# A banded-attention and feed-forward kernel on one core: the output projection one unit later, its weights 192 bytes into longer slots, and one pair of staging tiles less

## The chip, the core and the metric

The kernel runs on one core of a Trainium2 chip. The core has a matrix engine (TensorE, "PE" in the profile; its weight loads have a row of their own, "PEld"), a vector engine (VectorE, "DVE"), ScalarE ("ACT"), GpSimd ("POOL") and SyncE ("SP"). Each works through its own list of instructions in order and waits for others on semaphores. PE, ACT and DVE also reach PSUM, eight banks in which matmuls accumulate; everything else lies in SBUF, 128 partitions wide. Transfers are issued from the lists of SP, POOL and ACT.

The metric is the device time of one execution in microseconds (us).

## The reference

Sequence 2048, width 640 (32 heads of 20), feed-forward width 1536, all in float32.

```python
xn = _layernorm(x)
q, k, v = split(xn @ wqkv)                    # 32 heads of 20
idx = pos - [0, 2, 4, ..., 14]                # 8 earlier positions, every second one
logits = einsum(q, k[idx]) * 20 ** -0.5       # positions before the start are masked
s = (softmax(logits) . v[idx]) @ wo
g = silu(silu(xn @ w1) @ w2)
return x + s * g
```

## The kernel before

**Groups.** The 2048 positions are cut into four groups of 512: two halves of the sequence, and in each the even and the odd positions apart, since attention looks back in steps of 2. A group is T = 4 tiles of 128 positions.

**Precision.** Each float32 operand of a matmul is split into a high and a low part of the type fp32r, and a product is three matmuls: high by high, low by high, high by low. TH and TL hold the transposed activations' parts ([128, DC = 5, 512] each, two of each); a weight unit holds both parts side by side.

**Units.** The weights come as units, in the order of the list `units` (lines 277 to 287): per group 20 of `q` (NQ = 4 quarters of 8 heads, 5 chunks of 128 input rows; 480 columns), from the second group on 5 of `wo` (640 columns), then `w1` f and `w2` f - 1 alternating, f to 11 (`w1` is the stationary operand there; `w2` has 640 columns, and its stationary operand is SH/SL, the activated hidden units). The last group's `wo` comes at the end, in `wo_last`. `WR` is a ring of RING = 7 slots of 2 x 640 floats. Unit i lies in slot i % 7; `w_done` behind a unit's matmuls calls `w_load` (line 349) for the unit seven further on. When a unit comes for the first time (for half the `q` units the second time too), it is loaded raw by `raw_load` (line 315) into staging tiles (`RAW`, at first also `PR` and `G`), split by ACT and DVE or POOL, and stored in split form to DRAM; after that it is fetched in split form by a POOL transfer. `start` (line 311) gives the place in the slot at which a unit begins: QAT = 48 floats (192 bytes) for `q`, 0 else.

**A group's phases.** `qkv_phase` (line 624): four quarters of matmuls, 60 each; ACT copies their four banks out (lines 444, 447); transfers on SP fetch the earlier positions (halo, line 458); DVE does the scores (lines 481, 484 to 494) and the values (503 to 521), a backlog that goes on for the whole group. Between the quarters `o_chunk` transposes the previous group's attention output O into TH/TL (PE line 433, ACT 437, DVE 438), five chunks, at the places of O_AT. `wo_phase` (line 690) multiplies that by Wo: c = 0..4, and for each c the four tiles, in six PSUM banks: a[t] with 384 columns of tile t, b[t // 2] with the other 256 of two tiles. DVE multiplies the six banks into the gate G (line 704) in the order a0, a1, b0, a2, a3, b1; then four residual tiles are fetched into the two tiles XR by SP, POOL adds G (line 711), SP stores the result. `ffn_phase` (line 766): per f a W1 unit into one of two ROT banks (PE 791 to 793), ACT's silu twice (797, 798), DVE's low part (799), and the W2 unit of f - 1 into six banks (PE 672, 674 in `tm_mm`): first all tiles' products with SH, then those with SL. After the last f, ACT puts silu of the six banks into G (line 828). The six banks of `tm_banks` (line 663) are the same six in Wo and W2, in the same order; the quarters use them too.

In the last group the five chunks of O are transposed inside `ffn_phase`, ahead of the f of OL_AT, and `wo_last` (line 715) follows.

**The order.** It isn't the order of the program text. Every operation is handed to `Weave` with an engine, a price and a priority, and `Weave.order` plays the program through on its own clock: PE keeps its order, and on every other engine the next operation is, of those that can start first, the one with the lowest number as priority. L704 and L799 have 0, the attention work 100 and more. After the six operations of L704 the plan keeps DVE free for HOLD = 3.4 us; no instruction comes of that. The order that results is fixed in the instruction lists. A matmul of n columns is priced at `mm(n) = n / 2400 + 0.0155` us, so a Wo or W2 unit at 12 x (mm(384) + mm(256)).

Of the kernel before, what the change touches and what calls it, by code (L numbers as in the profile page):

```python
# [9 lines left out]
F32R = mybir.dt.float32r  # L10
# [4 lines left out]
P = 128  # L15
S, D, F, H, DH = 2048, 640, 1536, 32, 20
W = 8
DC, FC = D // P, F // P
# [15 lines left out]
HALVES = 1  # L34
BY_ACT = (1,)
QAT = 48
X_AT = 3, 6, 8
TILE_AT = 1, 1.5, 5, 6
LOW_AT = 3
# [134 lines left out]
def local_attention_silu_ffn(ctx: ExitStack, tc: tile.TileContext, x, wqkv, wo, w1, w2, out):  # L174
# [25 lines left out]
    ST = [sb.tile([P, 2, 6], F32, name="st0")]  # L200
    TH = tiles("th", 2, [P, DC, TOK], F32R)
    TL = tiles("tl", 2, [P, DC, TOK], F32R)
    WR = tiles("w", RING, [P, 2 * D], F32R)
    ST.append(sb.tile([P, 2, 6], F32, name="st1"))
    SH = tiles("sh", 2, [P, TOK], F32R)
    SL = tiles("sl", 2, [P, TOK], F32R)
# [11 lines left out]
    G = sb.tile([P, T, D], F32, name="gate")  # L218
    XR = tiles("xr", 2, [P, D])
    SF = tiles("sf", 2, [P, TOK])  # L220
    RAW = tiles("raw", 2, [P, D])
    ACC = [psum.tile([P, TOK], F32, name=f"acc{i}") for i in range(6)]
    ROT = [psum.tile([P, TOK], F32, name=f"rot{i}") for i in range(2)]
    carry = [dram.tile([2, NQ, 2, T, CQ], F32, name=f"carry{par}") for par in range(2)]
# [52 lines left out]
    units = []  # L277
    for g in range(NG):
        units += [("q", q, c) for q in range(NQ) for c in range(DC)]
        if g:  # L280
            units += [("wo", c) for c in range(DC)]
        for f in range(FC + 1):
            if f < FC:
                units.append(("w1", f))
            if f:
                units.append(("w2", f - 1))
    units += [("wo", c) for c in range(DC)]
# [22 lines left out]

    def start(u):

        return QAT if u[0] == "q" else 0

    def raw_load(k):


        if k >= len(fresh):
            return
        i = fresh[k]  # L320
        u = units[i]
        n = width(u)
        if k < DC:
            r, kr = PR.rearrange("p t w m -> p (t w m)")[:, k * n:(k + 1) * n], [PRK[k]]
        elif k < early:
            s = (k - DC) % 6
            r, kr = (RAW[s], [("raw", s)]) if s < 2 else (G[:, s - 2, :], [("g", s - 2, 0), ("g", s - 2, CA)])
            r = r[:, :n]
        else:
            s = k % 2  # L330
            r, kr = RAW[s][:, :n], [("raw", s)]
        raws[i] = r, kr
        if u[0] == "q":
            _, q, c = u
            src = wqkv[c * P:(c + 1) * P, :].rearrange("p (s m) -> p s m", s=3)[:, :, q * CQ:(q + 1) * CQ]
            dst = r.rearrange("p (s m) -> p s m", s=3)
        elif u[0] == "w1":
            src = w1.rearrange("(c p) f -> p c f", p=P)[:, :, u[1] * P:(u[1] + 1) * P]
            dst = r.rearrange("p (c f) -> p c f", c=DC)
        else:  # L340
            m = wo if u[0] == "wo" else w2
            src, dst = m[u[1] * P:(u[1] + 1) * P, :], r
        if k in BY_ACT:
            add("ACT", 0.65, lambda: nc.scalar.dma_start(dst, src), [], kr, -1, nbytes=n * P * 4)
            return
        dma(lambda: nc.sync.dma_start(dst, src), [], kr, n * P * 4, 1 + k if k < 2 * DC else clock[0] + 5,
            0.62 if k < 2 * DC else 0.45)

    def w_load():
        i = loaded[0]  # L350
        if i >= len(units):
            return
        loaded[0] += 1
        u, s = units[i], i % RING
        n = width(u)
        r = WR[s]
        at = start(u)
        both = r.rearrange("p (s d) -> p s d", s=2)[:, :, at:at + n]
        whi, wlo = both[:, 0], both[:, 1]
        kh, kl = ("wh", s), ("wl", s)  # L360
        due = clock[0]
        if what[i] == "load":
            src = halves[u]
            add("POOL", 1.0, lambda: nc.gpsimd.dma_start(both, src), [("half", u)], [kh, kl], due + 10,  # L364
                nbytes=2 * n * P * 4)
            return
        k = fresh.index(i)
        if not k:
            raw_load(0)
            rawn[0] = 1  # L370
        raw, kr = raws.pop(i)
        act(n, lambda: nc.scalar.activation(whi, raw, AF.Copy), kr + [("sd", 0)] * (k < 2), [kh], 1000 + due)
        pool_does = k < LO and k not in ON_DVE
        eng, cost, by = ("POOL", po(n), nc.gpsimd) if pool_does else ("DVE", dv(n), nc.vector)
        parts = HALVES if pool_does and k < DC else 1
        for j in range(parts):
            cs = slice(j * n // parts, (j + 1) * n // parts)
            add(eng, po(n // parts) if pool_does else cost, lambda cs=cs: by.tensor_tensor(
                out=wlo[:, cs], in0=raw[:, cs], in1=whi[:, cs].bitcast(F32), op=OP.subtract), [kh] + kr,
                [kl if j == parts - 1 else kl + (j,)], due if pool_does else LOW_AT if k < LO else 50, lock=True)  # L380
        if what[i] == "store":
            kept = dram.tile([P, 2, n], F32, name="half_" + "_".join(map(str, u)))
            halves[u] = kept
            dma(lambda: nc.sync.dma_start(kept, both.bitcast(F32)), [kh, kl], [("half", u)], 2 * n * P * 4,
                due + 25)
        while rawn[0] <= (min(k + 6, early - 1) if k < early - 2 else k + 2):
            raw_load(rawn[0])
            rawn[0] += 1
# [268 lines left out]
        return [(k, i, c, t) for k in kinds for c in cs for t in ts]  # L657

    O_AT = {(1, 1): 0, (1, 4): 1, (2, 3): 2, (3, 1): 3, (3, 3): 4}
    OL_AT = {8: 0, 9: 1, 10: 2, 11: 3, 12: 4}  # L660
    XT_AT = 7

    def tm_banks():
# [102 lines left out]
    def ffn_phase(g, i, ix, io):  # L766
        nxt = g + 1 if g + 1 < NG else None
        ps = prev = None
        for f in range(FC + 1):
            if nxt is not None and f == 0:  # L770
                load_x(nxt, 0, 2)
                load_x(nxt, 2, 2)
                for t in range(T):
                    ln_stats(t)
                ln_rstd(0, T)
                for t in range(T):
                    ln_apply(t)
            if nxt is not None and XT_AT <= f < XT_AT + DC:
                split_t(XIN, [("xin", t) for t in range(T)], f - XT_AT, ix)
            if nxt is None and f in OL_AT:  # L780
                o_chunk(g, OL_AT[f], io)
            cur = None
            if f < FC:
                wh, wl, kh, kl = w_next("w1", f)
                h, kp = rot()
                s = f % 2

                def first(wh=wh, wl=wl, h=h):
                    for c in range(DC):
                        cs = tsl(c)  # L790
                        nc.tensor.matmul(h, wh[:, cs], TH[i][:, c, :], start=c == 0, stop=False)  # L791
                        nc.tensor.matmul(h, wh[:, cs], TL[i][:, c, :], start=False, stop=False)  # L792
                        nc.tensor.matmul(h, wl[:, cs], TH[i][:, c, :], start=False, stop=c == DC - 1)  # L793
                pe(15 * mm(TOK), first, t_keys(i, range(DC)) + [kh, kl], [kp])
                w_done()
                sf, sh, sl = SF[s], SH[s], SL[s]
                act(TOK, lambda sh=sh, h=h: nc.scalar.activation(sh, h, AF.Silu), [kp], [("sh", s)], 0, "silu")  # L797
                act(TOK, lambda sf=sf, h=h: nc.scalar.activation(sf, h, AF.Silu), [kp], [("sf", s)], 0, "silu")
                dve(TOK, lambda sf=sf, sh=sh, sl=sl: nc.vector.tensor_tensor(  # L799
                    out=sl, in0=sf, in1=sh.bitcast(F32), op=OP.subtract), [("sf", s), ("sh", s)], [("sl", s)], 0, lock=True)  # L800
                cur = sh, sl, ("sh", s), ("sl", s)
            if f:
                sh, sl, ksh, ksl = prev
                if ps is None:
                    ps = tm_banks()
                a, b = ps
                wh, wl, kh, kl = w_next("w2", f - 1)
                for t in range(T):
                    def big(t=t, f=f, wh=wh, wl=wl, sh=sh):
                        tm_mm(ps, t, sh[:, tsl(t)], wh, f == 1, False)  # L810
                        tm_mm(ps, t, sh[:, tsl(t)], wl, False, False)

                    def small(t=t, f=f, wh=wh, sl=sl):
                        tm_mm(ps, t, sl[:, tsl(t)], wh, False, f == FC)
                    ko = [a[t][1], b[t // 2][1]]
                    pe(2 * TM, big, [ksh, kh, kl], ko)
                    if f == FC:
                        pe(TM, small, [ksl, kh], ko)
                    else:
                        late.append((TM, small, [ksl, kh], ko))  # L820
                for args in late:
                    pe(*args)
                late.clear()
                w_done()
            prev = cur
# [8 lines left out]
    for g in range(NG):  # L834
        other = 1 - slot
        qkv_phase(g, slot, other)
        if g:
            wo_phase(g - 1, other)
        ffn_phase(g, slot, other, other)
        if g < NG - 1:  # L840
            slot = other
# [30 lines left out]
```

## Time and profile before

| | |
|---|---|
| three runs | 641.08, 641.5, 641.52 us (median 641.5) |
| the profiled execution | 641.25 us, span of the profile 639.5 us |
| matrix engine busy | 632.2 us |
| vector engine busy | 540.1 us |
| ScalarE, GpSimd busy | 204.1, 122.3 us |
| read from and written to device memory | 109.55 MB, 34.16 MB |

The profile page gives busy times, a chain of waits that ends with the last instruction, and the costliest groups of instructions. Its trace can be cut into windows, where a row gives the length of the stretch, the busy time of an engine, its instructions in brackets, the granted clock of the matrix engine, and the share and rate of the transfers. The trace can also be listed in order of time: start, duration, engine, line of the kernel, operation, what it writes and reads, and, in square brackets, how long the engine was idle before it and what ended that. Matmuls overlap, so the pace is read from start to start, not from the duration of one.

### The profile page before, as it was taken

The page shows a single profiled execution, that of the slowest core. Times are in us where ns is not written, and L with a number is a line of the kernel's source. Part 1 is how long each engine was busy: PE and PEld are TensorE (multiplying, and loading weights), DVE is VectorE, ACT ScalarE, POOL GpSimd, SP SyncE. Part 2 cuts the span into 40 slices and gives each one's busy share as a digit, 9 for nine tenths or more (in the row PEclk, how much of TensorE's full clock was granted, in tenths as well). Part 3 has the DMA queues.
Part 4 walks back from the last instruction along what each step waited for, and adds up shares of the span by engine and source line. Part 5 has one row for each costly group of instructions (what it writes and reads, how often), then busy time and mean ns, then how long its engine had stood idle before and what let it go on. Part 6 is the DMA issues. An engine that isn't in the chain of part 4 may idle for free.

```text
span 639.5 us, 9016 instructions
## 1 busy us (share of the span) xinstructions
PE 632.2 (99%) x3495; PEld 572.2 (89%) x3495; DVE 540.1 (84%) x539; ACT 204.1 (32%) x399; POOL 122.3 (19%) x168
## 2 busy tenths in 40 slices
PE   7999999999999999999999999999999999999997
PEld 6888889999889989999888999999988899899997
DVE  7699999999999899999859999999106999999714
ACT  5436453443524023232422112223313222233230
POOL 4500000001101241111222124311222213311100
PEclk9999999999999999999999999999999999999999
DMA  9999998787999998657699976965679996876522
GB/s 283 336 307 337 338 372 327 298 280 237 280 285 327 318 310 258 197 163 218 179 270 272 297 214 207 359 201 162 171 207 265 276 315 202 284 272 189 183 83 82
DMA packets 74154, 162.44 MB, mean 254 GB/s; under 512 B 5648, under 2 KB 47088, under 8 KB 74112
## 3 DMA queue, kind: packets, MB, share of 16 engines
q0 software_dynamic: 26672, 82.58, 44.7%
q1 hardware_dynamic: 46896, 78.88, 39.6%
q8 instruction: 27, 0.44, 0.3%
q10 hardware_dynamic: 544, 0.41, 0.2%
q14 instruction: 15, 0.12, 0.1%
HBM read 109.55 MB, written 34.16 MB: 225 GB/s over the span
## 4 chain that ended last, share of the span: by engine, by line
PE 97%; DVE 1%; DMA 1%; ACT 0%; issue 0%
PE acc L672 22%; PE acc L674 15%; PE acc L638 10%; PE acc L639 10%; PE acc L640 10%; PE rot L793 9%; PE rot L791 9%; PE rot L792 9%; PE rot L433 2%; PE acc L583 2%; DMA xin<-in_A_x_dram 1%; DVE st L548 1%; DVE xin L553 0%; PE rot L761 0%; PE rot L562 0%; DVE tl L570 0%
## 5 line engine op out<-in xcount | busy, mean ns | idle before, releaser
L638 PE MATMUL acc<-w,th 128*128 128x480 f32 x300 | 114.7, 382 | 0.0
L672 PE MATMUL acc<-w,sh 128*128 128x384 f32 x384 | 113.6, 335 | 0.0
L639 PE MATMUL acc<-w,tl 128*128 128x480 f32 x300 | 113.5, 378 | 0.0
L640 PE MATMUL acc<-w,th 128*128 128x480 f32 x300 | 113.4, 378 | 0.0
L674 PE MATMUL acc<-w,sh 128*128 128x256 f32 x384 | 107.1, 279 | 0.0
L481 DVE TENSOR_TENSOR pr<-q,kv 128x2560 f32<-128x2560 f32 x32 | 90.3, 2821 | 11.7 <-DMA kv<-kv 11.3
L791 PE MATMUL rot<-th,w 128*128 128x512 f32 x240 | 95.4, 398 | 0.0
L793 PE MATMUL rot<-th,w 128*128 128x512 f32 x240 | 94.0, 391 | 0.0
L792 PE MATMUL rot<-tl,w 128*128 128x512 f32 x240 | 93.8, 391 | 0.0
L513 DVE TENSOR_TENSOR pr<-e,kv 128x2560 f32<-128x2560 f32 x32 | 90.3, 2823 | 0.8
L484 DVE TENSOR_REDUCE l<-pr 128x128 f32<-128x2560 f32 x32 | 90.0, 2813 | 0.2
L364 POOL DMA_DIRECT2D w<-half_q x52 | 37.3, 717 | 233.4 <-PE rot L793 122.5
L518 DVE TENSOR_TENSOR pr<-pr 128x1280 f32<-128x1280 f32 x64 | 78.3, 1224 | 1.1
L797 ACT ACTIVATE sh<-rot 128x512 fp32r<-128x512 f32 x48 | 28.8, 599 | 151.5 <-PE rot L793 151.4
L674 PEld LDWEIGHTS acc<-w,sh 128*128 128x128 f32 x384 | 72.3, 188 | 1.6
L672 PEld LDWEIGHTS acc<-w,sh 128*128 128x128 f32 x384 | 72.1, 188 | 1.7
L364 POOL DMA_DIRECT2D w<-half_w x72 | 38.5, 535 | 182.0 <-PE acc L674 89.9
L640 PEld LDWEIGHTS acc<-w,th 128*128 128x128 f32 x300 | 56.3, 188 | 8.5
L638 PEld LDWEIGHTS acc<-w,th 128*128 128x128 f32 x300 | 56.3, 188 | 8.0
L639 PEld LDWEIGHTS acc<-w,tl 128*128 128x128 f32 x300 | 56.3, 188 | 8.0
L672 PE MATMUL acc<-w,sl 128*128 128x384 f32 x192 | 57.8, 333 | 0.0
L793 PEld LDWEIGHTS rot<-th,w 128*128 128x128 f32 x240 | 45.0, 188 | 9.9
(88 smaller groups left out, 975.0 us busy)
## 6 DMA issues: line engine op xcount, KB each, us to landing
w<-half_w POOLq DMA_DIRECT2D x72, 640.0 KB, 5.7
w<-half_q POOLq DMA_DIRECT2D x52, 480.0 KB, 5.4
half_w<-w SPq DMA_DIRECT2D x24, 640.0 KB
half_q<-w SPq DMA_DIRECT2D x20, 480.0 KB
w<-half_wo POOLq DMA_DIRECT2D x15, 640.0 KB, 5.5
kv<-kv SPq DMA_DIRECT2D x16, 560.0 KB
kv<-kv SPq DMA_DIRECT2D x16, 420.0 KB
gate<-in_B_w_dram SPq DMA_DIRECT2D x16, 320.0 KB
```

The costliest lines, as they stand in the source:

```text
L481: dve(2560, lambda t=t: nc.vector.tensor_tensor(out=PR, in0=win(qq[:, t:t + 2, :], W, 0), in1=win(kv[:, 0, t:t + 2, :], W, CQ), op=OP.mult ...
L484: dve(2560, lambda t=t: nc.vector.tensor_reduce(out=l[:, t:t + 2].rearrange("p t w h -> p (t w h)"), in_=PR.rearrange("p t w (h d) -> p (t ...
L513: dve(2560, lambda t=t, v=v: nc.vector.tensor_tensor(out=PR.rearrange("p t w (h d) -> p t (w h) d", d=DH), in0=e[:, t:t + 2].rearrange("p ...
L518: dve(2 * n * CQ, lambda n=n: nc.vector.tensor_tensor(out=PR[:, :, 0:n, :], in0=PR[:, :, 0:n, :], in1=PR[:, :, n:2 * n, :], op=OP.add), [] ...
L638: nc.tensor.matmul(o, hi, wh, start=c == 0, stop=False)
L639: nc.tensor.matmul(o, lo, wh, start=False, stop=False)
L640: nc.tensor.matmul(o, hi, wl, start=False, stop=c == DC - 1)
L672: nc.tensor.matmul(a[t][0][:, :CA], st, w[:, :CA], start=first, stop=last)
L674: nc.tensor.matmul(b[t // 2][0][:, h * CB:(h + 1) * CB], st, w[:, CA:], start=first and h == 0, stop=last, skip_group_check=True)
L791: nc.tensor.matmul(h, wh[:, cs], TH[i][:, c, :], start=c == 0, stop=False)
L792: nc.tensor.matmul(h, wh[:, cs], TL[i][:, c, :], start=False, stop=False)
L793: nc.tensor.matmul(h, wl[:, cs], TH[i][:, c, :], start=False, stop=c == DC - 1)
```

## The change

The five Wo units move behind W1 unit 0 of the next feed-forward phase, in the list of units and in the phases: `wo_phase` is called inside `ffn_phase` when f is 0, after W1 unit 0 and its activations are handed to the plan. The slots of the ring get 64 floats more (256 bytes; 1792 over the ring, by which the tiles allocated behind it move), and a Wo unit begins 48 floats into its slot, as a `q` unit does already. The two tiles RAW are gone; raw weights are staged in XR, the tiles of the residual. In the last group the fourth chunk of O is transposed one step later (f = 12) and the fifth in the middle of the last W2 unit, before its third tile.

```diff
+WOAT = 48
+SLOT = 2 * D + 64
...
-    WR = tiles("w", RING, [P, 2 * D], F32R)
+    WR = tiles("w", RING, [P, SLOT], F32R)
...
-    RAW = tiles("raw", 2, [P, D])
...
         units += [("q", q, c) for q in range(NQ) for c in range(DC)]
-        if g:
-            units += [("wo", c) for c in range(DC)]
         for f in range(FC + 1):
             if f < FC:
                 units.append(("w1", f))
+            if g and f == 0:
+                units += [("wo", c) for c in range(DC)]
             if f:
                 units.append(("w2", f - 1))
...
-        return QAT if u[0] == "q" else 0
+        return QAT if u[0] == "q" else WOAT if u[0] == "wo" else 0
...
-            r, kr = (RAW[s], [("raw", s)]) if s < 2 else (G[:, s - 2, :], [("g", s - 2, 0), ("g", s - 2, CA)])
+            r, kr = (XR[s], [("xr", s)]) if s < 2 else (G[:, s - 2, :], [("g", s - 2, 0), ("g", s - 2, CA)])
...
-            r, kr = RAW[s][:, :n], [("raw", s)]
+            r, kr = XR[s][:, :n], [("xr", s)]
...
-        both = r.rearrange("p (s d) -> p s d", s=2)[:, :, at:at + n]
+        both = r[:, at:at + 2 * D].rearrange("p (s d) -> p s d", s=2)[:, :, :n]
...
-    OL_AT = {8: 0, 9: 1, 10: 2, 11: 3, 12: 4}
+    OL_AT = {8: 0, 9: 1, 10: 2, 12: 3}
...
                 cur = sh, sl, ("sh", s), ("sl", s)
+                if g and f == 0:
+                    wo_phase(g - 1, io)
...
                 for t in range(T):
+                    if nxt is None and f == FC and t == T // 2:
+                        o_chunk(g, DC - 1, io)
...
         qkv_phase(g, slot, other)
-        if g:
-            wo_phase(g - 1, other)
         ffn_phase(g, slot, other, other)
```

## The prediction

> **What bounds the kernel now.** I read the page's busy shares and its chain of waits first, then the matrix engine (PE) cut into windows at the borders of the phases that move, then the vector engine (DVE) around the same places in order of time.
>
> ```profile
> PE 632.2 (99%) x3495; PEld 572.2 (89%) x3495; DVE 540.1 (84%) x539; ACT 204.1 (32%) x399; POOL 122.3 (19%) x168
> ...
> PE 97%; DVE 1%; DMA 1%; ACT 0%; issue 0%
> ```
>
> PE is never out of work: 632.2 of 639.5 us, and 97% of the chain. So the time changes only where matmuls follow each other faster or slower, or where a matmul starts to wait. DVE, at 84%, is the only other engine near its limit.
>
> The stretch of group 2 that moves: first Wo unit, Wo units 2 to 5, W1 unit 0, W1 unit 1, W2 unit 0 (after the colon-separated borders: length, PE busy, matmuls, clock, DMA share, GB/s):
>
> ```profile
> 358.54:362.23 3.69, 3.69 (x25) 1.00 1.17 397
> 362.23:376.31 14.08, 14.08 (x98) 1.00 1.13 294
> 376.31:379.74 3.43, 3.43 (x18) 1.00 0.64 202
> 379.74:383.14 3.40, 3.40 (x17) 1.00 0.10 36
> 383.14:386.59 3.45, 3.45 (x25) 1.00 0.33 124
> ```
>
> The clock is 1.00 throughout. A Wo unit takes 14.08/4 = 3.52 us, its first one 0.17 us more. A W2 unit, with the same 24 matmuls of 384 and 256 columns, takes 3.45. The same work, then, has two paces. Group 3 has the same shape; its Wo starts at 515.22 and its first W2 at 539.80. The last row is group 1 from Wo's end to its first W2:
>
> ```profile
> 515.22:518.92 3.70, 3.70 (x25) 1.00 1.07 335
> 518.92:533.00 14.08, 14.08 (x98) 1.00 0.99 285
> 533.00:539.80 6.80, 6.80 (x32) 1.00 0.44 139
> ...
> 219.65:226.45 6.80, 6.80 (x32) 1.00 0.84 276
> ```
>
> Now DVE beside these, groups 1, 2 and 3 (start, length, instruction):
>
> ```profile
> 218.94 3.14 DVE L704 TENSOR_TENSOR gate<-acc,gate 128x384 f32<-128x384 f32 x6
> ...
> 380.20 3.14 DVE L704 TENSOR_TENSOR gate<-acc,gate 128x384 f32<-128x384 f32 x6
> 383.26 0.77 DVE L799 TENSOR_TENSOR sl<-sf,sh 128x512 fp32r<-128x512 f32 x1
> 383.95 2.81 DVE L484 TENSOR_REDUCE l<-pr 128x128 f32<-128x2560 f32 x1
> ...
> 535.45 3.14 DVE L704 TENSOR_TENSOR gate<-acc,gate 128x384 f32<-128x384 f32 x6
> ...
> 540.71 2.81 DVE L484 TENSOR_REDUCE l<-pr 128x128 f32<-128x2560 f32 x1
> ```
>
> L704 is the multiplication that empties Wo's six banks. In group 2 Wo ends at 376.31, yet L704 starts only at 380.20, 3.89 us later; in group 3 at 533.00 and 535.45, 2.45 later; in group 1 before the end (219.65). DVE isn't idle in between: it works through an order that was fixed at build time by a plan in which PE is slower. The plan prices a W2 unit at 12 x (mm(384) + mm(256)) = 12 x 0.298 = 3.57 us, and the row above says 3.45. Over a group PE gets ahead of the plan, and whatever the plan put ahead of L704 then makes the banks late. Today this is harmless: the next user of the banks is the first W2 unit, two W1 units (6.83 us) behind Wo's end.
>
> **The change part by part.**
>
> *Wo's entry.* Today Wo's banks are those of the last quarter, and Wo waits for ScalarE to copy them out:
>
> ```profile
> PEld acc L674 <- ACT q L447: 0.8, 3, 0.3
> ...
> 62.94:66.37 3.43, 3.43 (x17) 1.00 1.12 364
> ```
>
> The first Wo unit is 0.17 to 0.18 us over the others, three times. With W1 unit 0 (own banks, 3.43 us) between, the copies are long done. W1 directly behind a quarter is what group 0 has: 3.43 (second row) against 3.40, so 0.03 is paid back. Sum: 3 x (-0.18 + 0.03) = **-0.45 us**.
>
> *The 192 bytes.* No added instruction; only the address at which the moving matrix starts against the stationary one. From the tile sizes in the code, W2's stationary tile lies 64 bytes (the small statistics tile between, rounded up) past a multiple of 256 from its weights, and for a quarter, whose weights start 192 in, the stationary tile is again 64 past a multiple of 256. Wo alone of the three sits at 0. That Wo has W2's shapes but not its pace fits. The bounds: W2's 3.45, and above it the slowest the same shapes ever run, the last W2 unit:
>
> ```profile
> 614.32:618.00 3.68, 3.68 (x27) 1.00 0.00 0
> ```
>
> Per phase of five units that is -0.35 to +0.80. I take -0.35, the row whose address relation Wo gets: four phases, **-1.40 us**.
>
> The Trainium skill speaks against it: SBUF — State Buffer, "Who interferes with whom", gives PE two independent read ports, one for the moving operand and one for weight loads, and says PE never waits on anyone for SBUF. By that rule the offset is worth 0. Here Wo and W2 differ by 2% at equal shapes and clock, which the rule does not explain, but nothing yet shows that the address is the reason.
>
> *The longer slots* move every second slot by 256 bytes against a multiple of 512, for W1, W2 and the quarters too. I take 0, since the relation modulo 256 is kept everywhere; the other end is among the rivals.
>
> *Wo's move: DVE.* This carries the forecast. In the plan Wo's sums are done one W1 unit, 3.43 us, later. Of DVE's work only one piece moves ahead of L704 with it: L799 of W1 unit 0, 0.69 us at a free engine. So the plan has 3.43 - 0.69 = 2.74 us more of waiting before L704 can be issued, and fills it from the attention work, in pieces of 2.81 us: in groups 2 and 3 the next in line is L484 (383.95, 540.71). However long the plan waited before (anything from 0 to one piece), one L484 goes ahead, unless it waited nearly a whole piece already. On the chip none of that is waited for, since PE is ahead; DVE simply reaches L704 later: 380.20 + 0.69 + 2.81 = 383.70 in group 2, 535.45 + 3.50 = 538.95 in group 3. Both places hang on PE's time, because DVE starts each of these groups by waiting for the halo of its first quarter:
>
> ```profile
> 330.98 2.83 DVE L481 TENSOR_TENSOR pr<-q,kv 128x2560 f32<-128x2560 f32 x1 [6.40 <-DMA kv<-kv]
> ...
> 485.84 2.83 DVE L481 TENSOR_TENSOR pr<-q,kv 128x2560 f32<-128x2560 f32 x1 [4.58 <-DMA kv<-kv]
> ```
>
> so a loss in group 2 doesn't save group 3 from its own. What is late next: W2 unit 0 is now one W1 unit behind Wo. Its order of need is a0, b0 (short matmul, 0.18 us in), later b1 (2 x 4 matmuls, 1.15 us, after b0); DVE's order is a0, a1, b0, a2, a3, b1. b0 is done half way, 1.57 us into L704, b1 at 3.14.
>
> Group 2: PE reaches b0 at 358.54 + 3.43 + 5 x 3.45 + 3.40 + 0.18 = 382.80; b0 is ready at 383.70 + 1.57 = 385.27: 2.47 us. b1 is wanted at 385.27 + 1.15 = 386.42 and ready at 386.84: 0.42. Together 2.89. Group 3: 515.22 + 3.43 + 17.25 + 3.58 = 539.48 against 538.95 + 1.57 = 540.52: 1.04, and 0.42 again: 1.46. Group 1: L704 slips by at most 0.69 + 2.74 + a piece, from 218.94 to 225.2 at the very latest, with b0 at 226.8; b0 is wanted at 226.45 - 0.15 - 0.35 + 0.18 = 226.1. The next pieces there are shorter (1.48, below), so some 223 is likelier: 0, at worst 0.7. Sum: **+4.35 us**. Lower end 0, if the plan finds no piece to put ahead; upper end: PE further ahead by another 0.5.
>
> Queued behind the waiting matmuls is all of PE, so nothing hides this.
>
> *Wo's move: POOL and SP.* Per group five weight loads, five stores once, four residual loads, adds and stores change place. POOL's order holds a weight load behind the residual adds, which wait for L704:
>
> ```profile
> 381.90 3.56 POOL L711 TENSOR_TENSOR xr<-xr,gate 128x640 f32<-128x640 f32 x2 [4.59 <-DVE gate L704]
> 385.41 1.10 POOL L364 DMA_DIRECT2D w<-half_w  x2
> ...
> w<-half_w POOLq DMA_DIRECT2D x72, 640.0 KB, 5.7
> ```
>
> L704 3.5 us later holds them 3.5 us longer. A load is issued seven slots ahead, six units of 3.4 us or more, 20 us, and lands in 5.7: 14 us of cover. 0; without that cover up to 3.5 per group.
>
> *Raw weights in XR.* The last raw tile is read at 206.17 and the first residual add is at 222.43; one unit later each, they stay apart. 0.
>
> ```profile
> 206.17 0.83 DVE L378 TENSOR_TENSOR w<-raw,w 128x640 fp32r<-128x640 f32 x1 [0.29 <-ACT w L372]
> ...
> 222.43 3.10 POOL L711 TENSOR_TENSOR xr<-xr,gate 128x640 f32<-128x640 f32 x2
> ```
>
> *The last two transposes* (five as before): one stood before a W1 unit, which then took 3.52 instead of 3.45; one before the last W2 unit, which took 3.68. Now both split the last W2 unit: 0.23 a piece at worst, +0.16 in all; since each slows only half a unit, 0.
>
> ```profile
> 606.99:610.51 3.52, 3.52 (x18) 1.00 0.64 195
> ```
>
> Sum: -0.45 - 1.40 + 4.35 = +2.50. The profiled execution took 641.25 us (span 639.5 and 1.75 around it), 0.25 under the median of the runs, 641.5. **641.25 + 2.50 = 643.8 us.**
>
> **Rivals.**
> - *No wait (the other side).* The plan had nearly waited a piece already, or holds DVE free for Wo's sums, and L704 goes right behind L799: 380.20 + 0.69 = 380.89, b0 at 382.46, before PE wants it at 382.80. Then 641.25 - 0.45 - 1.40 = **639.4**. It decides from where L704 starts in group 2 earlier than 382.80 - 1.57 = 381.2. For it: the plan prefers L704 to all attention work as soon as it can start. Against: the 3.89 us of today.
> - *Wo keeps its pace.* Then the waits shrink by 0.35 each, to 2.54 and 1.11, and -1.40 falls away: 641.25 - 0.45 + 3.65 = **644.5**. By the skill's two ports this is the likelier one.
> - *The slots' 256 bytes count.* If W2 runs at 3.68 in every second slot, 24 units x 0.23 = 5.5 more: **649**. For it: W2 has shown that pace; against: only behind transposes, in one place.
> - *Waits and gains cancel*, because the piece put ahead is a short one, as L518 in group 1 (1.48):
>
> ```profile
> 226.02 1.48 DVE L518 TENSOR_TENSOR pr<-pr 128x1280 f32<-128x1280 f32 x1
> ```
>
> L704 at 382.37, b0 at 383.94: 1.14 and 0.42; in group 3 only b1, 0.13. 641.25 - 1.85 + 1.69 = **641.1**. Against: no L518 is next in line in groups 2 and 3.
>
> **How the numbers follow.** Forecast 0.41, Wo's old pace 0.18, no wait 0.24, cancel 0.10, slots 0.07. A measurement of this kernel can tell 0.2%, 1.3 us, from no change. Slower (over 642.8): 0.41 + 0.18 + 0.07 = 0.66; the same 0.10; faster (under 640.2) 0.24. The range takes in the no-wait case and Wo's slow bound (+0.80 a phase cuts the waits to 1.74 and 0.3: 641.25 - 0.45 + 3.20 + 2.04 = 646.0): 639.3 to 646.0. The likeliest one's own range is 642.8 to 645.5.
>
> **What would show it.** In the changed profile: two PE waits on DVE's L704 at the first W2 unit of groups 2 and 3, 2 to 3 and 1 to 2 us, none in group 1; one L484 more ahead of L704; Wo units at 3.45; no wait for L447 at Wo's entry; W1, W2 and quarter units at 3.40 to 3.45 and their old pace. Wrong if L704 starts within 2 us of Wo's end in group 2, or if W2's units have two lengths.

## The result and the profile after

| | before | after |
|---|---|---|
| median of 12 runs (us) | 641.22 (640.95 to 642.86) | 642.60 (642.23 to 644.04) |
| ratio, 95% interval | | 1.0023 (1.0015 to 1.0031) |
| profiled execution, span (us) | 641.25, 639.5 | 642.30, 640.5 |

The change costs 1.4 us in the median and 1.0 in the profiled pair. The forecast was 643.8, 2.5 over the kernel before: the direction is right and the time lies inside the stated range (639.3 to 646.0), but 0.2 below the likeliest case's own range (642.8 to 645.5). The profile shows that the kernel gets there another way than was forecast.

First the busy line of the page of after:

```profile
PE 633.2 (99%) x3495; PEld 573.8 (90%) x3495; DVE 535.4 (84%) x539; ACT 211.8 (33%) x405; POOL 126.1 (20%) x168
```

Then all that the matrix engine (PE) waited for in after (line that waited and its releaser; us in all, times, longest):

```profile
PE rot L563 <- DVE xin L554: 1.8, 3, 0.9
PE rot L537 <- POOL ident masks.py:199: 1.4, 1, 1.4
PE acc L584 <- DVE tl L571: 0.3, 1, 0.3
```

PE's busy time is 1.0 us up (632.2 to 633.2), as much as the span, and its three waits are those of the program's start. No wait for the vector engine (DVE) at a W2 unit is among them. So the forecast's stall isn't there, and matmuls run slower somewhere. The windows of PE in after tell where: Wo in group 1; W1 unit 0, Wo, W1 unit 1, W2 unit 0 of group 2; Wo in group 3; Wo's last part (the matmuls of `wo_last`):

```profile
205.25:223.24 17.99, 17.99 (x121) 1.00 1.05 345
...
358.78:362.22 3.44, 3.44 (x16) 1.00 1.19 366
...
362.22:380.22 18.00, 18.00 (x122) 1.00 1.04 278
380.22:383.66 3.44, 3.44 (x17) 1.00 0.04 12
383.66:387.11 3.45, 3.45 (x25) 1.00 0.40 121
519.19:537.19 18.00, 18.00 (x122) 1.00 0.99 267
618.77:634.92 16.15, 16.15 (x107) 1.00 0.11 42
```

And the last part before:

```profile
618.00:633.83 15.83, 15.83 (x107) 1.00 0.11 42
```

A Wo phase was 17.77 (3.69 + 14.08), its entry wait of 0.18 included; now it is 18.00 without one. The last part went from 15.83 to 16.15. W2 unit 0 has its old 3.45, at full clock. Three phases by 0.22 and the last part's 0.32 make 0.98, about the difference of the spans.

Inside the phase, in after (start, length, instruction). A pair is a matmul of 384 columns and one of 256, and its pace, from here on, is the time from one start of L673 to the next:

```profile
362.22 0.34 PE L673 MATMUL acc<-w,th 128*128 128x384 f32 x1
362.40 0.28 PE L675 MATMUL acc<-w,th 128*128 128x256 f32 x1
362.52 0.34 PE L673 MATMUL acc<-w,th 128*128 128x384 f32 x1
...
363.42 0.34 PE L673 MATMUL acc<-w,th 128*128 128x384 f32 x1
```

Four pairs in 1.20 us: 300 ns a pair, where before it was 3.52/12 = 293. Wo did get W2's address relation, but not the 287 ns (3.45/12) of W2.

DVE around L704 in group 2, first the piece ahead of it in before, then after, where the line is L705, in groups 2 and 3:

```profile
377.46 2.83 DVE L481 TENSOR_TENSOR pr<-q,kv 128x2560 f32<-128x2560 f32 x1
```

```profile
378.64 2.83 DVE L482 TENSOR_TENSOR pr<-q,kv 128x2560 f32<-128x2560 f32 x1
381.38 3.14 DVE L705 TENSOR_TENSOR gate<-acc,gate 128x384 f32<-128x384 f32 x6
384.44 2.81 DVE L485 TENSOR_REDUCE l<-pr 128x128 f32<-128x2560 f32 x1
...
537.74 3.14 DVE L705 TENSOR_TENSOR gate<-acc,gate 128x384 f32<-128x384 f32 x6
```

The L481 that stood ahead of L704 still stands there as L482, and the next L485 is behind L705 (384.44): none was put in. L705 starts at 381.38 in group 2, 1.16 us behind Wo's end, not 3.89.

### The profile page after: what moved, and what is told of

It reads as the page before. It is cut to its first block, busy times and chain, and to the rows that moved or that the text cites. A ratio compares the mean times of both kernels' runs of the same rounds, so it can differ in the third digit from the quotient of the medians.

```text
span 640.5 us, 9029 instructions
## 1 busy us (share of the span) xinstructions
PE 633.2 (99%) x3495; PEld 573.8 (90%) x3495; DVE 535.4 (84%) x539; ACT 211.8 (33%) x405; POOL 126.1 (20%) x168
## 4 chain that ended last, share of the span: by engine, by line
PE 97%; DVE 1%; DMA 0%; ACT 0%; issue 0%
PE acc L673 22%; PE acc L675 15%; PE acc L640 10%; PE acc L639 10%; PE acc L641 10%; PE rot L794 9%; PE rot L792 9%; PE rot L793 9%; PE rot L434 2%; PE acc L584 2%; DVE st L549 1%; DMA xin<-in_A_x_dram 0%; DVE xin L554 0%; PE rot L762 0%; PE rot L563 0%; DVE tl L571 0%
## 5 line engine op out<-in xcount | busy, mean ns | idle before, releaser
L673 PE MATMUL acc<-w,sh 128*128 128x384 f32 x384 | 113.7, 335 | 0.0
L482 DVE TENSOR_TENSOR pr<-q,kv 128x2560 f32<-128x2560 f32 x32 | 90.3, 2821 | 12.9 <-DMA kv<-kv 12.6
L514 DVE TENSOR_TENSOR pr<-e,kv 128x2560 f32<-128x2560 f32 x32 | 91.8, 2869 | 0.6
L485 DVE TENSOR_REDUCE l<-pr 128x128 f32<-128x2560 f32 x32 | 90.0, 2813 | 0.4
L673 PEld LDWEIGHTS acc<-w,sh 128*128 128x128 f32 x384 | 72.1, 188 | 1.7
L673 PE MATMUL acc<-w,sl 128*128 128x384 f32 x192 | 57.8, 333 | 0.0
L439 DVE TENSOR_TENSOR tl<-rot,th 128x512 fp32r<-128x512 f32 x35 | 23.9, 683 | 39.6 <-ACT th L438 39.5
```

Source lines behind the costliest of these rows:

```text
L482: dve(2560, lambda t=t: nc.vector.tensor_tensor(out=PR, in0=win(qq[:, t:t + 2, :], W, 0), in1=win(kv[:, 0, t:t + 2, :], W, CQ), op=OP.mult ...
L485: dve(2560, lambda t=t: nc.vector.tensor_reduce(out=l[:, t:t + 2].rearrange("p t w h -> p (t w h)"), in_=PR.rearrange("p t w (h d) -> p (t ...
L514: dve(2560, lambda t=t, v=v: nc.vector.tensor_tensor(out=PR.rearrange("p t w (h d) -> p t (w h) d", d=DH), in0=e[:, t:t + 2].rearrange("p ...
L673: nc.tensor.matmul(a[t][0][:, :CA], st, w[:, :CA], start=first, stop=last)
```

## The experiments

Three parts of the change could slow Wo: the start of its weights, its place behind a W1 unit, and the longer slots. The first experiments take them apart, one tests the stall that didn't come, and the later ones follow the two paces that turned up.

Times are medians, with the ratio to the kernel before, run beside it on the same chip; "one run" marks the time of a single run. All of them lie within 1% of the kernel before, so the pace of the phases in the profiles says more than the times. "Start" is the bytes by which Wo's weights begin inside their slot, and the entry of a phase is how its first matmuls begin behind what ran before.

| version | us | ratio (95%) | Wo phases, last part (us) |
|---|---|---|---|
| start 0 | 640.82 | 0.9996 (0.9984 to 1.0008) | 17.60, 15.81 |
| Wo in its old place, start 192 | 640.90 | 0.9986 (0.9976 to 0.9997) | 17.91, 18.15, 18.15, 16.14 |
| start 0, old slot length | 640.75 | 0.9998 (0.9988 to 1.0007) | 17.60, 15.81 |
| start 64 | 642.8, one run | | 17.60, 15.80 |
| PATIENCE 0.8 | 644.9 | 1.0063 (1.0036 to 1.009) | 17.99, 16.15 |
| short matmul first in the phases | 640.92, one run | | 17.20, 16.15 |
| a start of its own for each unit | 647.3, one run | | mixed |
| short first in the last part too | 639.43 | 0.9971 (0.9960 to 0.9982) | 17.20, 15.51 |
| old place, short first | 640.87 | 0.9988 (0.9979 to 0.9998) | 17.31, 16.14 |
| start 0, short first | 641.96, one run | | 17.60, 15.82 |
| short first, last transposes as before | 642.28, one run | | 17.20, 16.14 |
| old place, short first, transposes of after | 640.23 | 0.9984 (0.9973 to 0.9994) | 17.31, 15.51 |

### Start 0

```diff
-WOAT = 48
+WOAT = 0
```

> The changed kernel with one number put back: Wo's weights start at 0 of their slot again; the longer slots, the new place and XR stay. Theory A (the start of 192 bytes itself slows Wo's matmuls): a Wo phase goes back from 18.00 us to 5 x 3.52 = 17.6, four phases 1.6 us, so about 641.0 against 642.6, and 0.2 to 0.5 under the kernel before, since the wait at Wo's entry is gone. Theory B (Wo's place behind a W1 unit brings the slow pace): the phases stay at 18.00, 642.6. Theory C (the longer slots): as B.

Measured: 640.82. The windows of this version's PE, Wo in group 1 and the last part:

```profile
205.18:222.78 17.60, 17.60 (x122) 1.00 1.08 347
...
617.39:633.20 15.81, 15.81 (x108) 1.00 0.11 42
```

With nothing but the start undone, the phase is at 293 ns a pair again (17.60/60) and the last part at 15.81. So it is the start that costs 0.40 a phase and 0.34 in the last part, 1.54 us in all; the place and the slots are still those of after.

### Wo in its old place, with the start of 192

```diff
-                if g and f == 0:
-                    wo_phase(g - 1, io)
...
+        if g:
+            wo_phase(g - 1, other)
         ffn_phase(g, slot, other, other)
```

(and the same in the list of units, and the last transposes as before)

> The changed kernel with Wo and the two transposes put back in their old places; the start of 192 bytes, the longer slots and XR stay. A: the Wo phases take 18.0 and the entry wait of 0.18 on top, about 18.2; 1.6 us over the kernel before, 642.8. C: the same. B: 17.78 as before, 641.2.

Measured: 640.90, nearest to the 641.2 of B and 1.9 under the 642.8 of A and C. But the runs go from 639.96 to 642.16, and the profiled one is the slowest of them; the phases of the others may have been shorter, which no trace shows. Its phases in groups 1 and 2 (group 3 is as group 2):

```profile
201.59:219.50 17.91, 17.47 (x121) 1.00 1.08 326
358.40:376.55 18.15, 18.15 (x121) 1.00 1.13 308
```

The same code at the same addresses has two paces. In group 1 PE stood still for 0.44 (17.91 less 17.47), and yet the phase is the shortest; two of its pairs against two of group 2, in the time order of PE of this version:

```profile
210.04 0.33 PE L673 MATMUL acc<-w,th 128*128 128x384 f32 x1
...
210.61 0.33 PE L673 MATMUL acc<-w,tl 128*128 128x384 f32 x1
...
366.05 0.34 PE L673 MATMUL acc<-w,th 128*128 128x384 f32 x1
...
366.65 0.34 PE L673 MATMUL acc<-w,th 128*128 128x384 f32 x1
```

570 ns for two pairs in group 1 (some 287 each), 600 in group 2. What the trace shows to differ is the entry: the first two starts of L673 lie 1.00 us apart in group 1, where PE waited for ScalarE's copies, and 0.46 in groups 2 and 3.

### Start 0 and the old slot length; start 64

```diff
-WOAT = 48
-SLOT = 2 * D + 64
+WOAT = 0
+SLOT = 2 * D
...
```

(and the view of a slot as before)

> The changed kernel with Wo's start at 0 and slots of the old length; only the new place and XR are left of the change. A: as with the start alone put back, 17.6 us a phase and about 641.0. C: here too 17.6 and 641.0, but only here, not with the start alone put back. B: 18.00 and 642.6.

Measured: 640.75 beside the 640.82 of the long slots, with the same phases. The 256 bytes cost nothing, and they bring nothing by themselves: they are the room for the start. Since the longer slots move every second unit by 256 bytes against this version, and the phases don't change, 256 bytes more or less don't count for the pace.

```diff
-WOAT = 48
+WOAT = 16
```

> The changed kernel with Wo's start at 64 bytes in place of 192. A says only that the pace depends on the start: 17.25 to 18.4 us a phase, not 18.00 by chance. B and C: 18.00. If what counts is that stationary and moving tile lie 64 bytes apart modulo 256, either way round, 18.00 too; if the sign counts, another number.

Measured: phases of 17.60 and a last part of 15.80, 293 ns a pair, "another number" than 18.00. So the side to which the two tiles lie apart counts. The one run of 642.8 was at a clock of 0.997 and began Wo 1.9 us later than after (207.11), so its time says nothing of the change.

### PATIENCE 0.8

The plan orders DVE's work at build time, and it has a rule that the description of the order above leaves out. Where it would start a piece of low urgency, and an urgent one can start within PATIENCE us (or half the piece, if that is shorter), it leaves DVE idle for the urgent one:

```python
if pick.prio >= 140:
    ...
            if o.prio < 100 and t <= m + min(self.PATIENCE, pick.dur / 2)]
```

```diff
-    PATIENCE = 1.0
+    PATIENCE = 0.8
```

> The changed kernel with PATIENCE 0.8 in place of 1.0, by which the plan no longer holds DVE free for Wo's sums, and one L485 (L484 before) stands ahead of L705 (L704 before) in groups 2 and 3, as the prediction had it; PE's order is the same. If the prediction priced that right: L705 starts near 384.2 in group 2 and 540.6 in group 3 where it now starts at 381.4 and 537.7; PE waits at the first W2 unit, 1.5 to 3 us and 0.8 to 2; in all 2.5 to 4.5 us over the changed kernel's 642.3. If the banks are free in time all the same: 642.3.

Measured: 644.9 in the median of three runs (644.22 to 646.35), 2.3 over after; the profiled one is the slowest. DVE and PE of this version in group 2:

```profile
379.41 2.83 DVE L482 TENSOR_TENSOR pr<-q,kv 128x2560 f32<-128x2560 f32 x1
382.27 2.82 DVE L485 TENSOR_REDUCE l<-pr 128x128 f32<-128x2560 f32 x1
385.01 3.14 DVE L705 TENSOR_TENSOR gate<-acc,gate 128x384 f32<-128x384 f32 x6
```

```profile
384.43 0.39 PE L794 MATMUL rot<-th,w 128*128 128x512 f32 x1
385.66 0.41 PE L673 MATMUL acc<-w,sh 128*128 128x384 f32 x1 [0.84 <-issue]
386.68 0.38 PE L675 MATMUL acc<-w,sh 128*128 128x256 f32 x1 [0.60 <-DVE gate L705]
```

Now the L485 stands ahead of L705, in group 3 too, and PE waits: 384.43 to 385.66 where 0.23 is usual, 1.00 us; then 385.66 to 386.68 where 0.18 is usual, 0.84. For the first wait the trace names no releaser ("issue"); it falls where a0, the first bank that L705 frees, is wanted. In all, this version's first W2 unit of group 2 takes 4.84 instead of 3.45 behind that 1.00, and that of group 3 4.18: 1.00 + 1.39 + 0.73 = 3.1 us. (This execution's span is 4.1 over after's; the other 1.0 was lost ahead of the first Wo phase, which begins at 206.25 and not 205.25.) That is the stall that was forecast. What kept it away in after is the rule above: since 1.0 keeps L485 back and 0.8 doesn't, the time for which the plan leaves DVE idle there lies between the two.

### Every unit its own start

```diff
-        return QAT if u[0] == "q" else WOAT if u[0] == "wo" else 0
+        if u[0] == "q":
+            return (0, 16, 32, 48, 64)[u[2]]
+        if u[0] == "wo":
+            return (8, 24, 32, 40, 56)[u[1]]
+        return (0, 8, 16, 24, 32, 40, 48, 56, 4, 12, 20, 28)[u[1]]
```

> The changed kernel with every unit at a start of its own, in bytes: q by chunk 0, 64, 128, 192, 256; Wo by chunk 32, 96, 128, 160, 224; W1 and W2 by f 0, 32, 64 and so on to 224, then 16, 48, 80, 112. It maps the pace against the distance between stationary and moving tile. If only the distance modulo 256 counts: q at 0 and at 256 alike, and W2 at two starts with the same distance alike. If addresses don't matter at all: one pace for each kind of unit (q 216 ns a matmul, W1 3.45, W2 3.45, Wo 3.60 us), whatever the start.

The windows of PE are units of group 2: Wo at 32 and 128 bytes, then W2 at 0, 64, 96 and 192 (24 matmuls each, so a pair is a twelfth):

```profile
365.40:368.90 3.50, 3.50 (x25) 1.00 1.03 264
372.41:376.02 3.61, 3.61 (x27) 1.00 1.37 312
...
386.55:390.00 3.45, 3.45 (x25) 1.00 0.68 192
400.52:404.04 3.52, 3.52 (x25) 1.00 0.94 287
407.53:411.03 3.50, 3.50 (x25) 1.00 0.99 325
428.95:432.53 3.58, 3.58 (x26) 1.00 0.55 163
```

By the tile sizes in the code, and counted from the start of a slot, Wo's stationary tile lies at 0 modulo 256 and W2's at 64. Take the distance, stationary less moving modulo 256: Wo at 32 and W2 at 96 both have 224, and both take 3.50; Wo at 128 and W2 at 192 have 128, 3.61 and 3.58; W2 at 64 has the 0 that Wo had before, and takes 3.52 as Wo did then. Equal distances give equal paces within 0.03 us a unit, over different tiles and units; the distances of 32, 96 and 160, all at 3.51 or 3.52, agree with that. W2 at 0 has a distance of 64, and so has Wo at 192. (The expectation for the quarters isn't clearly met: their units at 0 take 216.2 to 216.7 ns a matmul and those at 256 217.7 to 218.0, where in after, with one start for all, the same two take 215.7 to 215.9 and 216.3 to 216.4. That 256 bytes don't count rests on the slots, not on them.)

### Short matmul first

At a distance of 64 the entry chooses between two paces. This version turns the order within each pair of the three phases: 256 columns, then 384.

```diff
+        if short:
+            nc.tensor.matmul(b[t // 2][0][:, h * CB:(h + 1) * CB], st, w[:, CA:], start=first and h == 0,
+                             stop=last, skip_group_check=True)
+            nc.tensor.matmul(a[t][0][:, :CA], st, w[:, :CA], start=first, stop=last)
+            return
...
```

> The changed kernel, but in wo_phase each pair of matmuls issues its 256 columns ahead of its 384; wo_last is as it was. If the slow pace (182 and 118 ns) is one of two in which the same addresses can run, and the entry decides, then the three inner phases may fall into 171 and 116, 17.3 us in place of 18.0; if addresses alone give 300 ns a pair, 18.0 again, and 16.15 in wo_last in both cases.

Measured: all three phases at 17.20, 287 ns a pair. The last part, whose order was left, stays at 16.15. PE then stopped at two W2 stretches of this execution, one in group 1 (7.75 us instead of 6.89) and the first unit of group 2 (3.82 instead of 3.45; at its fifth pair, where the banks a2 and b1 are first wanted). The first, in the time order of PE:

```profile
300.79 0.28 PE L680 MATMUL acc<-w,sh 128*128 128x256 f32 x1
301.64 0.44 PE L678 MATMUL acc<-w,sl 128*128 128x384 f32 x1 [0.58 <-DVE sl L805]
```

And in that of DVE, same version:

```profile
298.16 2.83 DVE L514 TENSOR_TENSOR pr<-e,kv 128x2560 f32<-128x2560 f32 x1
300.90 0.69 DVE L805 TENSOR_TENSOR sl<-sf,sh 128x512 fp32r<-128x512 f32 x1
```

The next version, which differs in the order of the last part's matmuls alone, has no such wait: there this L514 starts at 296.18, and DVE is idle for 0.81 us ahead of L805. What made DVE 2 us later in this execution is open.

### Short first in the last part too

```diff
-    tm_mm(banks, t, st, ws[c][k == 1], k + c == 0, k == 2 and c == DC - 1, cols)
+    tm_mm(banks, t, st, ws[c][k == 1], k + c == 0, k == 2 and c == DC - 1, cols, short=len(cols) == 2)
```

> The kernel after with the short matmul (256 columns) ahead of the long one in every pair of Wo, in the three phases and now in the last part too. Theory "entry" (at 64 bytes from the stationary matrix to the weights two paces exist, 287 and 300 ns a pair, and the order of the first matmuls chooses): the last part enters the pace of 287 as the phases did, 105 matmuls or 52 pairs x 13 ns = 0.68 us less than 16.15, so some 15.5; the phases stay at 17.20, and the waits on DVE that the faster Wo uncovered (0.37 at the first W2 unit of group 2, 0.86 in group 1) stay about as they were: about 640.2 us. Rival "place": the last part, entered from W2 and not from W1, stays at 300 ns and 16.15, whatever its order: about 640.9.

Measured: 639.43 (639.24 to 640.51 in 7 runs), the lowest median of all, 0.3% under the kernel before. The theory had 640.2, with waits for DVE that this execution doesn't have. Group 2 and the last part in this version's windows:

```profile
361.55:378.75 17.20, 17.20 (x121) 1.00 1.01 277
...
616.50:632.01 15.51, 15.51 (x107) 1.00 0.12 43
```

Against after that is 3 x 0.80 + 0.64 = 3.04 us less of Wo, and the median is 3.17 lower (the two were not run side by side).

### The same in the old place; and at start 0

The old-place version above and the start-0 version, each with the short matmul first in the phases and in the last part.

> Wo in its old place ahead of W1 unit 0, its weights 192 bytes in, the short matmul first in every pair. Theory "entry by order": all three phases at 287 ns a pair, 17.20 us and 0.1 to 0.3 for ScalarE's copies at the entry, so 17.3 to 17.5 against 17.78 of the kernel before; the last part 15.5 against 15.83; no wait for DVE at the first W2 unit, which is two W1 units behind: 641.2 - 3 x 0.35 - 0.35 = 639.8 us, and runs that scatter less than with the long matmul first. Rival "entry by the wait": what chose the pace was the interruption at ScalarE's copies, and with it phases come out at 300 as well as 287, up to 18.15: 640 to 642, scattered.

Measured: 640.87, where the theory had 639.8. The phases come out alike, 17.31, so the order chooses the pace even behind a wait; but the last part stays slow, which is 0.64 of the miss:

```profile
359.04:376.36 17.32, 17.32 (x121) 1.00 1.08 304
...
617.86:634.00 16.14, 16.14 (x108) 1.00 0.11 42
```

The rest of it isn't explained; the profiled execution (641.4) began its first Wo phase at 202.58, 0.7 later than the kernel before.

> The kernel after with Wo's weights at 0 and the short matmul first everywhere. Theory "distance": at a distance of 0 modulo 256 there is one pace, and the order doesn't matter: 293 ns a pair, phases of 17.6 us, the last part 15.8. Rival "order": short first is faster by itself, whatever the addresses: 287 ns, phases of 17.2 us, the last part 15.5.

Measured: 17.60 and 15.82. At a distance of 0 the order of the matmuls changes nothing: it doesn't make the pair faster, it only chooses between the paces of the distance of 64.

### What chose the last part's pace

Two versions with the short matmul first: Wo in after's place with the last transposes as before, and Wo in its old place with the transposes of after (in the middle of the last W2 unit).

```diff
-    OL_AT = {8: 0, 9: 1, 10: 2, 12: 3}
+    OL_AT = {8: 0, 9: 1, 10: 2, 11: 3, 12: 4}
...
-                    if nxt is None and f == FC and t == T // 2:
-                        o_chunk(g, DC - 1, io)
```

(the first version's; the second leaves these lines as in after and puts Wo back as in the old-place version)

> The version with the short matmul first in the phases and in the last part (place of after), with the last two groups of transposes where the kernel before has them: one ahead of the second last W1 or W2 unit and one ahead of the whole last W2 unit, none in its middle. Theory "halves": the last part came into the pace of 287 only because the transposes in the middle of the last W2 unit shift where it begins; without them it runs at 300, 16.15 us, and the last W2 unit takes 3.68. Rival "place": the last part is at 287, 15.5 us, wherever the transposes stand, and 16.14 in the version with Wo in its old place has another reason.

> Wo in its old place ahead of W1 unit 0, 192 bytes in, short matmul first everywhere, and the last transposes in two halves as in after: all of the version that was fastest but the move of Wo. Theory "halves": the phases 17.31 us, the last part 15.5, so 640.87 - 0.64 = 640.2 us, and if the runs are as the profile, about 641.3 - 3 x 0.47 - 0.32 = 639.6; then the move of Wo is worth no more than its entry, 3 x 0.11 us. Rival "place": the last part stays at 16.14 us, 640.9.

Measured, the last part in the windows of the first version, then of the second:

```profile
618.75:634.89 16.14, 16.14 (x108) 1.00 0.11 42
```

```profile
617.40:632.91 15.51, 15.51 (x107) 1.00 0.12 43
```

So it is the transposes: the last part comes into 287 only with the short matmul first and the transposes inside the unit ahead of it; either alone leaves 300, wherever the phases stand. The transposes also change what runs just ahead: where they stand ahead of the whole last W2 unit, that unit runs at 300 ns a pair (3.68); where they split it, its second half runs at 287 (1.81). With the short matmul first the last part kept the pace that ran ahead of it, in all four versions; with the long one first it was 300 behind either. (The first version's single run, 642.28, also holds two waits for DVE, one of them 1.1 us at the transposes, so its time doesn't compare.)

The second version's median is the expected one (640.23 for 640.2), but the move is worth more than was allowed: 640.23 beside 639.43, spans of 638.5 and 637.5, for three entries by 0.11. Its PE at the border from the last quarter to Wo in group 2:

```profile
358.20 0.37 PE L641 MATMUL acc<-w,th 128*128 128x480 f32 x1
358.65 0.39 PE L673 MATMUL acc<-w,th 128*128 128x256 f32 x1
358.87 0.34 PE L675 MATMUL acc<-w,th 128*128 128x384 f32 x1
```

The wait for ScalarE's copies now falls in two places: 0.45 where 0.22 is usual for a quarter's matmul, and 0.22 where 0.12 is usual for the short one. That is 0.33 a group, more than the 0.18 of the kernel before; probably because a short matmul in front wants the bank of the 256 columns sooner. So with this order the move is worth some 0.8 us (3 x 0.33, less 3 x 0.05 for the W1 units); the intervals of the two ratios overlap (0.9960 to 0.9982, and 0.9973 to 0.9994).

## Why the prediction came out near, and where it was wrong

The sum said -0.45 - 1.40 + 4.35 = +2.50. The two profiles say -0.39 + 1.54 + 0 and some 0.1 less elsewhere: +1.0. Two terms were wrong in opposite directions, so that the time came near is luck. The prediction's own sign of being wrong came true, too: "if L704 starts within 2 us of Wo's end in group 2"; it starts 1.16 behind. And 642.60 lies just under the 642.8 from which the prediction counted a time as slower; only the cancelling rival, with 0.10, had put it between 640.2 and 642.8.

- **Wo's entry, -0.45: right.** No first pair of 0.45 is left in after (the phase is 60 even pairs), which is 3 x 0.18; W1 units 0 and 1 paid 0.05 a group back (3.44 + 3.44 beside 3.43 + 3.40), where 0.03 was allowed. -0.39.
- **The 192 bytes, -1.40: the sign was wrong.** The failed step is "I take -0.35, the row whose address relation Wo gets". That the relation sets the pace was right, and so was which relation Wo gets; but W2's row isn't the only pace at it. Start 0 puts the cost at +1.54, 0.40 a phase, well inside the bound of +0.80. The other pace stood in the trace of before, in the very unit from which that bound was taken. PE in that last W2 unit and in W2 unit 0 of group 2, before:

```profile
615.60 0.34 PE L672 MATMUL acc<-w,sh 128*128 128x384 f32 x1
...
617.10 0.34 PE L672 MATMUL acc<-w,sh 128*128 128x384 f32 x1
...
384.30 0.33 PE L672 MATMUL acc<-w,sh 128*128 128x384 f32 x1
...
385.44 0.33 PE L672 MATMUL acc<-w,sl 128*128 128x384 f32 x1
```

  Five pairs in 1.50 us are 300 ns each, four in 1.14 are 285, at one address relation and one shape. The 3.68 was read as a unit that transposes had held up; it was a unit at the slow pace throughout (12 x 0.30, and 0.1 at its first pair), and the two rows together would have said that the relation alone promises nothing.
- **By the Trainium skill's two ports** (SBUF — State Buffer, "Who interferes with whom": two independent read ports, and PE waits for no one) the offset was worth 0. The runs don't agree: 287, 292, 293 and 300 ns for the same pair, by nothing but a start address or an entry. The measurement decides. No run shows by what the addresses act.
- **Wo's move, DVE, +4.35: 0.** The failed step is "one L484 goes ahead, unless it waited nearly a whole piece already". The plan doesn't only start or fill; it may leave DVE idle for up to PATIENCE us, and the version with 0.8 shows that here it did. L704 came 1.18 us later in group 2 (380.20 to 381.38) and 2.29 in group 3, not 3.50. In group 1 it came 3.24 later (218.94 to 222.18) without a wait, as forecast. The price itself was about right: with 0.8 for PATIENCE the L485 stands there, and PE loses 2.4 us in group 2 and 0.7 in group 3, against 2.89 and 1.46 at a Wo pace that would have brought PE there 0.75 earlier (5 x 0.15).
- **The no-wait rival held** in its mechanism, "holds DVE free for Wo's sums", and missed its own line by little: L705 at 381.38, where 381.2 was to decide. The slower Wo, which brought PE to its first W2 unit at 383.66 and not 382.62, covered that and part of what b1 would have cost. In the two executions where Wo ran at 287 and L704 was nearly as late (381.09, and 381.08 with the last transposes as before), PE did stop at that unit's fifth pair, where b1 is wanted: 3.82 and 3.67 us for 3.45, beside the 0.42 of the sum. In a third, with L704 at 379.35, it didn't. The rival failed as a time, 639.4, by the 192 bytes that it had taken over.
- **The slots, 0: right** (640.75 beside 640.82). The rival at 649 falls.
- **POOL and the queues, raw weights in XR, the last transposes, 0: right.** PE's only wait for POOL is the one at the program's start, W2's last unit takes 1.88 + 1.81 beside 3.68. That these two halves change how Wo's last part can be entered nobody priced; it is worth 0.64 once the order is turned.

## What to carry to other kernels

Before an address relation is copied from a fast loop to a slow one, look for all the paces that the fast loop itself shows, in units that follow something else than usual: a second pace there means that the entry decides too, and the order of the first matmuls is then a cheap thing to try. Where an order is fixed by a plan, look up every rule by which it may hold an engine idle before forecasting what it fills a gap with; a threshold such as PATIENCE can be worth more than the piece that is moved (here 3.1 us against a piece of 2.81). And when a sum comes out near the measured time, check its terms: here two errors, of 2.94 and of 4.35 us, took most of each other away.

## What the runs showed of the hardware

- The pace of the same pair of matmuls (384 and 256 columns, a weight load each) depends on the distance of the stationary and the moving matrix modulo 256 bytes: 293 ns at 0 and at 192, 292 at 224, 298 to 301 at 128, 287 or 300 at 64. Equal distances gave equal paces for Wo and W2, within 0.03 us a unit of twelve pairs.
- At 64 both paces held through the 120 matmuls of a Wo phase. Entered by the long matmul behind a W1 unit it was 300 in six phases of six (two versions), entered by the short one 287 in nine of nine (three versions); behind the wait at a quarter's end the long one came into either within one execution, the short one into 287 in six of six. At 0 there was one pace for both orders. Why the entry decides is not shown by any run here.
- A stop in the middle of a unit can change the pace at 64 as well. In the two units of 3.82 and 3.67 us the fourth pair was at 285 and 286 ns, and behind the stop at the fifth the last pairs were at 300; transposes in the middle of the last W2 unit took it from 300 to 287. In the version at start 0 with the old slots, the first W2 unit of group 3 (3.52 us) had its fourth pair at 286 ns and its last three at 300, with no wait in the trace.
